# Infini-attention with an FNet layer: the 16 slots of an attention group in another order, odd heads' probabilities in three tiles, and projection maxima taken from SBUF copies

## The chip, the cores and the metric

The kernel runs on one core of a Trainium2 chip. The metric is the device time of one execution in microseconds (us); less is better. Three runs of the kernel before gave 1058.62, 1060.83 and 1062.48 us; the median is 1060.83 us.

## The reference

Two layers on separate inputs, joined along the last axis. A is an Infini-attention with 32 heads of 18 features over four segments of 512 rows; B is a Fourier mixing layer, four dense products. Cut to what is computed:

```python
def _A_ref(x, wq, wk, wv, wo, beta):              # x [1, 2048, 576]
    q, k, v = (per head and segment) x @ wq, x @ wk, x @ wv
    for s in range(4):
        p = softmax(q_s k_s^T * scale + mask)     # 512 x 512, lower triangle
        a_dot = p @ v_s
        a_mem = phi(q_s) @ M / (phi(q_s) @ z + 1e-6)
        o_s = g * a_mem + (1 - g) * a_dot
        M, z = M + phi(k_s)^T v_s, z + sum(phi(k_s))
    return concat(o) @ wo
def _B_ref(x, ...):                               # x [1, 2048, 576]
    a, b = x @ hid_re^T, x @ hid_im^T
    return seq_re @ a - seq_im @ b
return concat([A, B], axis=-1)                    # [1, 2048, 1152]
```

## The kernel before

**Precision.** Most float32 operands are split into a high and a low part (`hi` = a rounded copy made by ACT, `lo` = the difference made by DVE or POOL), and products are the sum of three matmuls, hi·lo, hi·hi and lo·hi.

**Three stages.** First the four segments are projected (`project_qk` for nine 128-row blocks m = 0 to 3, 8, 4 to 7; then `project_v`, `k_natural` and `lookup`), and q, k and v go to DRAM, scaled and cut into two float16 parts. Then comes the attention stage: 32 groups G of four heads (two "halves" of two heads; x = 0 is the even head of a half, x = 1 the odd one) are worked off by the generator `attention()`, and between its pieces the dense work of layer B is put. Last comes the output product.

**Order.** Nothing is scheduled by a compiler: each engine runs its instructions in the order in which the Python code emits them, and waits on semaphores where data or buffers are not there. `later(n, fn)` emits a piece n ticks afterwards. In the projection there is one tick after each block m and each row tile j of v. In the attention stage `attention()` yields 16 times in each step g; each yield is a slot. After a slot's pieces come a tick and a portion of dense work (`dense()`), so many matmuls that the dense work is spread evenly over 34 steps of 16 slots. `on(lag, fn)` calls a piece for group g - lag, so each step holds pieces of three groups.

**The dense work** is fed in chunks of 128x512. `c_load` (L473) loads a chunk with a DMA on SP's queue, `c_cut` (L481) makes `chi` on ACT and, a tick later, `clo` on POOL (L493), two chunks ahead of their use by the matmuls of L631. There are 160 chunks, five to a step.

**A group of heads.** The even heads are computed with keys on the partitions (`t_fill`, `t_exp`, `t_mask`, `t_hi`, `t_lo`: probabilities come out ready for the product with v); they need the row maxima beforehand (`scores(.., 0, ..)`, `s_min`, `maxima`, `maxima_turn`, `maxima_out`, which ends in the small DMA `st<-mt` on SP's queue). The odd heads are computed with queries on the partitions (`scores(.., 1, ..)`, `f_min`, `f_exp`), cut into `hl` (`f_hi` on ACT, `f_lo`), and turned by a transposing DMA on SP's queue (`f_turn`, L1073), before the product with v (`pv`). Rows of 128 queries come in three kinds, `ROWS`: kind 0 is row block 3 (512 keys), kind 1 blocks 0 and 2 (128 and 384), kind 2 block 1 (256).

**Buffers that tie the order.** Scores live in two pairs of PSUM banks, `s` and `t` (`banks`, L1011), used in turn by four blocks of score matmuls in a step; a block has to wait until the readers of the last one are through. `hl`, the float16 tile [128, 2, 1280] of one half's odd head, has `bufs=2`, and a group takes two of them, one for each half: a group's first `f_hi` writes where the group before was, and so waits for that group's `f_turn` to have been read by the DMA. The code that takes it is

```python
        if len(hl) == half:
            hl.append(sa.tile([P, 2, 1280], F16, name="hl", bufs=2))
```

SP's queue issues in order as well: `st<-mt`, the loads of a later group (`stack_load`, four DMAs; `value_load`, one), `c_load`, the stores, and `f_turn`.

**Projection.** `project_qk` (L287) copies a block from PSUM to SBUF on ACT (`x`, L300), lets DVE take the largest magnitude of each row from PSUM (`largest`, L258), and for queries of segments 1 to 3 goes on with `phi` on the same PSUM bank (ACT L217, L218; DVE L220, L221; POOL L222). One tick later `scales` (POOL, L264 to L269) makes a power of two from the maxima, and two or three ticks later `cut_scaled` cuts the block: for keys ACT L278 and DVE L279, for queries ACT L274, L275 and POOL L276; a tick later `keep` issues the two DMAs to DRAM.

Of the kernel before, what the change touches and what calls it, by code (L numbers as in the profile page):

```python
# [24 lines left out]
P = 128  # L25
# [13 lines left out]
def infini_attention_and_fnet(ctx: ExitStack, tc: tile.TileContext, xT, wqk, w8, wv, wo, beta, xtT, cT, hT, out):  # L39
# [231 lines left out]
    def cut_scaled(x, scale, engine):  # L271
        p = sb.tile([P, 2, L], F16, name="p", tag="p", bufs=5)
        if engine is pool:
            act.activation(x, x, AF.Copy, scale=scale)  # L274
            act.activation(p[:, 0], x, AF.Copy)  # L275
            pool.tensor_tensor(p[:, 1], x, p[:, 0], OP.subtract)  # L276
        else:
            act.activation(p[:, 0], x, AF.Copy, scale=scale)  # L278
            dve.scalar_tensor_tensor(p[:, 1], x, scale, p[:, 0], op0=OP.mult, op1=OP.subtract)  # L279
        return p  # L280
# [6 lines left out]
    def project_qk(s, m):  # L287
# [13 lines left out]
        if m < 8:  # L301
            largest(o, MX[m % 4][:, m // 4:m // 4 + 1])
        else:
            t = sb.tile([P, 1], F32, name="mt", bufs=1)
            MX[4] = y = sb.tile([P, 2], F32, name="mx", bufs=5)
            largest(o, t)
# [3 lines left out]
        if m >= 4:  # L310
# [15 lines left out]
            later(2, low)  # L326
            if m < 8:
                later(3, low_query)
# [678 lines left out]
    ROWS = (((3, 0),), ((0, 384), (2, 0)), ((1, 0),))  # L1007
# [41 lines left out]
    def f_exp(G, kind):  # L1049
        nb, _, _, o, g = F_[G]  # L1050
        o = o.pop(kind)
        if kind == 2:
            g += [sa.tile([P, 768], F32, name="pg", bufs=2) for _ in BOTH]
        rows = [i for i, _ in ROWS[kind]]
        b = nb.rearrange("p (h n) -> p h n", h=2)[:, :, rows[0]:rows[-1] + 1:max(1, rows[-1] - rows[0])]
        act.activation(b, b, AF.Copy, bias=LIFT)  # L1056
        for half in BOTH:
            for i, c in ROWS[kind]:
                w = (i + 1) * P
                act.activation(f_cols(G, half, FIRST_COL[i], w), o[half][:, c:c + w], AF.Exp,  # L1060
                               bias=nb[:, 4 * half + i:4 * half + i + 1], scale=-1.0)

    def f_hi(G, half, a, b):
        hl = F_[G][2]
        if len(hl) == half:
            hl.append(sa.tile([P, 2, 1280], F16, name="hl", bufs=2))
        act.activation(hl[half][:, 0, a:b], f_cols(G, half, a, b - a), AF.Copy)

    def f_lo(G, half, engine, a, b):
        hl = F_[G][2]  # L1070
        engine.tensor_tensor(hl[half][:, 1, a:b], f_cols(G, half, a, b - a), hl[half][:, 0, a:b], OP.subtract)  # L1071

    def f_turn(G, half):  # L1073
        PT[G, 1, half] = sa.tile([P, 20, P], F16, name="ptt", bufs=2)
        nc.sync.dma_start_transpose(PT[G, 1, half], F_[G][2][half].rearrange("p a c -> p (a c)"))
# [23 lines left out]
    def t_fill(G, kind, o):  # L1099
        q, k = ST[G % NST]  # L1100
        if kind == 0:
# [110 lines left out]
    def attention():  # L1212
# [3 lines left out]
        for g in range(STEPS):  # L1216
# [4 lines left out]
            for half in BOTH:  # L1221
                on(1, f_hi, half, 512, 1280)
                on(2, t_lo, half, 2, pool)
# [3 lines left out]
            on(0, scores, 1, 0, b)  # L1227
            on(0, scores, 0, 0, a)
            on(2, pv, 1, 1)
            on(0, f_min, 0, b)  # L1230
            on(0, s_min, 0, a)
# [153 lines left out]
```

## Time and profile before

| | |
|---|---|
| profiled execution | 1060.17 us |
| span of its instructions | 1058.0 us |
| median of three other runs | 1060.83 us |
| mean granted TensorE clock | 0.980 |
| DMA traffic | 181.65 MB, 64.4% of 16 engines' span |
| busy in the eight stretches of 22 us from 249 to 425 us, mean of one | PE 21.53, DVE 14.47, ACT 16.33, POOL 14.75 us |

PE is the matmul engine, PEld its weight loads, DVE, ACT and POOL are the vector, scalar and GpSimd engines, SPq is the queue from which SP issues DMAs. A matmul's recorded duration overlaps the next one's, so PE's busy time says when it had work, not how fast it went. The profiled execution lies 0.66 us under the median, and 2.17 us of it lie outside the span.

A line of a timeline gives the start (us), the time (us), engine, line and operation, then output and inputs, and in brackets how long the engine had been idle and what ended it. A line of the waits gives who waited for whom, the total (us), how often, and the longest. A line of the stages gives the stretch, its length, each engine's busy time and instructions, then the granted clock, the DMA engines' share and GB/s.

### The profile page before, as it was taken

How to read it: one execution, taken by the hardware profiler on the slowest of the kernel's cores; microseconds unless marked ns; L12 is line 12 of the kernel's file. 1: busy time of each engine (PE TensorE's matmuls, PEld its weight loads, DVE VectorE, ACT ScalarE, POOL GpSimd, SP SyncE). 2: the span in 40 equal slices, each digit the busy share in tenths (PEclk: the TensorE clock that was granted, in tenths of full speed). 3: DMA queues.
4: the chain of work that ended last, by engine and by line, in shares of the span. 5: the costliest groups of instructions: out<-in, count | busy, mean ns of one | idle time of the engine just before them, and what ended most of it. 6: DMA issues, size and time to landing. Idle time of an engine off the chain costs nothing.

```text
span 1058.0 us, 25597 instructions
## 1 busy us (share of the span) xinstructions
PE 997.1 (94%) x9246; PEld 898.9 (85%) x9246; DVE 697.5 (66%) x1965; ACT 707.8 (67%) x1612; POOL 706.1 (67%) x984
## 2 busy tenths in 40 slices
PE   9998989978999999999898999998989899999998
PEld 8987979878888888888787889987878788888998
DVE  7756757567666566556666667776556667675675
ACT  6856558466787677766777778867656577667342
POOL 0656656467568766776767878866777788777561
PEclk9998999989999999999999999999999999999999
DMA  6524415355556976788757786567798678887463
GB/s 218 181 92 139 160 38 213 114 173 179 139 148 168 201 177 160 166 206 200 181 160 188 181 204 179 158 167 177 196 207 225 175 186 184 203 189 197 116 199 124
DMA packets 282974, 181.65 MB, mean 172 GB/s; under 512 B 204864, under 2 KB 239808, under 8 KB 282816
## 3 DMA queue, kind: packets, MB, share of 16 engines
q1 hardware_dynamic: 282624, 179.88, 64.4%
q8 instruction: 72, 1.18, 0.5%
q14 instruction: 54, 0.44, 0.1%
q10 hardware_dynamic: 224, 0.14, 0.0%
HBM read 94.06 MB, written 44.83 MB: 131 GB/s over the span
## 4 chain that ended last, share of the span: by engine, by line
PE 41%; ACT 17%; POOL 15%; DVE 14%; issue 10%; DMA 2%; POOLq 0%; SPq 0%; DVEq 0%; ACTq 0%
PE d L631 13%; POOL clo L493 5%; ACT pg L1060 4%; DVE s L1031 4%; PE qk L249 4%; POOL hl L1071 4%; PE v L82 2%; PE d L676 2%; PE d L677 2%; PE s L1023 2%; PE d L678 2%; DVE hl L1071 2%; PE t L918 2%; PE pv L1153 2%; DVE plo L1136 2%
## 5 line engine op out<-in xcount | busy, mean ns | idle before, releaser
L493 POOL TENSOR_TENSOR clo<-craw,chi 128x512 fp32r<-128x512 f32 x159 | 209.2, 1317 | 136.4 <-ACT chi L488 130.7
L1031 DVE CUSTOM_DVE_ANT_0 s<-s,causal 128x128 f32<-128x128 f32 (+2 forms) x448 | 203.2, 482 | 146.9 <-PE s L1023 142.5
L631 PE MATMUL d<-wide,chi 128*128 128x288 f32 x1408 | 257.8, 300 | 4.4 <-ACT y L699 3.1
L631 PEld LDWEIGHTS d<-wide,chi 128*128 128x128 f32 x1408 | 211.2, 191 | 5.8 <-ACT y L699 4.1
L631 PE MATMUL d<-wide,clo 128*128 128x288 f32 x704 | 167.3, 304 | 4.9 <-POOL clo L493 4.9
L631 PEld LDWEIGHTS d<-wide,clo 128*128 128x128 f32 x704 | 117.4, 191 | 6.7 <-POOL clo L493 6.6
L631 PE MATMUL d<-ab,chi 128*128 128x288 f32 x640 | 122.6, 302 | 0.0
L488 ACT ACTIVATE chi<-craw 128x512 fp32r<-128x512 f32 x160 | 100.9, 632 | 7.3 <-PE d L631 5.3
L1071 POOL TENSOR_TENSOR hl<-pg,hl 128x768 f16<-128x768 f32 x64 | 104.9, 1662 | 1.1 <-DMA st<-kd 0.8
L631 PEld LDWEIGHTS d<-ab,chi 128*128 128x128 f32 x640 | 99.7, 193 | 0.0
L1120 ACT ACTIVATE pd<-t 128x384 f32<-128x384 f32 (+1 forms) x128 | 64.6, 531 | 38.3 <-PE t L1109 38.0
L631 PE MATMUL d<-ab,clo 128*128 128x288 f32 x320 | 82.2, 306 | 2.4 <-POOL clo L493 2.3
L1023 PE MATMUL s<-st 54*128 54x256 f16 (+3 forms) x448 | 61.8, 290 | 24.0 <-ACT pg L1060 22.8
L1116 ACT ACTIVATE phi<-t 128x384 f16<-128x384 f32 x128 | 60.8, 475 | 29.1 <-PE t L1109 29.0
L1060 ACT ACTIVATE pg<-s,nb 128x128 f32<-128x128 f32 (+1 forms) x192 | 77.1, 474 | 2.1
L676 PE MATMUL d<-wide,chi 128*128 128x288 f32 x256 | 77.8, 304 | 0.5 <-DVE wide L92 0.3
L677 PE MATMUL d<-wide,chi 128*128 128x288 f32 x256 | 75.7, 296 | 0.0
L678 PE MATMUL d<-wide,clo 128*128 128x288 f32 x256 | 75.6, 295 | 0.0
L1129 ACT ACTIVATE phi<-pd 128x512 f16<-128x512 f32 x64 | 40.3, 629 | 48.8 <-POOL pd L1124 48.5
L1056 ACT ACTIVATE nb<-nb 128x2 f32<-128x2 f32 (+1 forms) x96 | 20.1, 210 | 61.4 <-DVE nb L1031 61.2
L82 PE MATMUL v<-wide,xh 128*128 128x288 f32 x256 | 56.9, 315 | 4.3 <-DVE mx L258 4.3
L1136 POOL TENSOR_TENSOR plo<-pd,phi 128x384 f16<-128x384 f32 x64 | 60.2, 961 | 0.6
(298 smaller groups left out, 2708.8 us busy)
## 6 DMA issues: line engine op xcount, KB each, us to landing
craw<-cT SPq DMA_DIRECT2D x128, 256.0 KB
craw<-xtT SPq DMA_DIRECT2D x32, 320.0 KB
vd<-vs SPq DMA_DIRECT2D x16, 440.0 KB
vst<-vd SPq DMA_DIRECT2D x32, 220.0 KB
st<-qd SPq DMA_DIRECT2D x64, 108.0 KB
st<-kd SPq DMA_DIRECT2D x64, 108.0 KB
yd<-y SPq DMA_DIRECT2D x16, 288.0 KB
y<-yd SPq DMA_DIRECT2D x16, 288.0 KB
```

Source lines behind the costliest of these rows:

```text
L82: pe.matmul(o, a, b, start=n == 0, stop=n == len(terms) - 1)
L488: act.activation(hi, raw[:, :4], AF.Copy)
L493: engine.tensor_tensor(lo, raw[:, :4], hi.bitcast(F32), OP.subtract)
L631: pe.matmul(o[h], a, b[:, h * 288:h * 288 + 288], start=start, stop=stop)
L676: pe.matmul(o, xh[:, k], wl[k][:, cs], start=k == 0, stop=False)
L677: pe.matmul(o, xh[:, k], wh[k][:, cs], start=False, stop=False)
L678: pe.matmul(o, xl[:, k], wh[k][:, cs], start=False, stop=False)
L1023: pe.matmul(o[half][:, first + c:first + c + w], q[r, x, i * P:w], k[r, x, :w], start=True, stop=True)
L1031: dve.tensor_tensor_reduce(x, x, CAUSAL[0][:, L - w:], scale=scale, scalar=-LOWEST, op0=OP.add, op1=OP.min, accum_out=into[:, 4 * half + i ...
L1060: act.activation(f_cols(G, half, FIRST_COL[i], w), o[half][:, c:c + w], AF.Exp, bias=nb[:, 4 * half + i:4 * half + i + 1], scale=-1.0)
L1071: engine.tensor_tensor(hl[half][:, 1, a:b], f_cols(G, half, a, b - a), hl[half][:, 0, a:b], OP.subtract)
L1136: engine.tensor_tensor(lo[:, a:b], f, hi[:, a:b], OP.subtract)
```

## The change

Three things are changed. In the projection, `largest` reads the SBUF copy `x` in place of the PSUM bank; `cut_scaled` emits the high part at once and the low part with its DMAs a tick later; and the cut is emitted three ticks after the block (keys had two) in segments 0 to 2, and two ticks after it (queries had three) in segment 3. In the attention stage, the odd heads' probabilities get three float32 tiles by kind (`pf1`, 512 columns; `pf0`, 512; `pf2`, 256) in place of two (512 and 768), with one `f_hi` and one `f_lo` for each kind and half; in kind 1 the row blocks are taken in the other order. And the pieces of a group stand in other slots (the number in brackets is the lag; h is a half):

| slot | before | after |
|---|---|---|
| 0 | f_hi 512:1280 (1), t_lo 2 (2) | t_lo 2 (2) |
| 1 | scores odd 0 and even 0, pv odd h1 (2), f_min 0, s_min 0 | scores odd 1 and even 0, f_min 1, s_min 0, t_hi h0 (2) |
| 2 | f_exp 0, pv_read odd (2), f_lo 512:1280 on POOL (1) | f_turn h0 (1), t_hi h1 (2), pv_out odd (2) |
| 3 | pv_out odd (2) | f_turn h1 (1), f_exp 1, t_lo 0 h0 (2) |
| 4 | f_turn h0 (1) | f_hi 1, t_lo 0 h1 (2) |
| 5 | scores even 1, t_fill 0 (1), pv even h0 (2), s_min 1, t_exp 0 (1) | f_lo 1 on POOL |
| 6 | f_turn h1 (1), t_mask (1) | scores odd 0 and even 1, pv even (2), f_min 0, s_min 1 |
| 7 | - | memory_load (1) |
| 8 | t_hi h0 (1), memory_load (1) | f_exp 0 |
| 9 | scores even 2 and odd 2, t_fill 1 (1), pv even h1 (2), s_min 2, t_exp 1 and t_lo 1 (1), f_min 2, pv_read even (2) | f_hi 0 |
| 10 | maxima, f_exp 2, t_hi h1 and t_lo 0 h0 (1) | scores even 2 and odd 2, t_fill 1 (1), s_min 2, f_min 2, t_exp 1 (1) |
| 11 | pv_out even (2), f_hi 0:512, t_lo 0 h1 (1) | maxima, f_exp 2, t_lo 1 (1), pv_read even (2) |
| 12 | f_lo 0:512 on DVE | f_hi 2, pv_out even (2) |
| 13 | scores odd 1, t_fill 2 (1), maxima_turn, pv odd h0 (1), f_min 1, maxima_out, t_exp 2 (1) | f_lo 2 on POOL, f_lo 0 on DVE |
| 14 | f_exp 1, stack_load, value_load | t_fill 0 and 2 (1), pv odd (1), maxima_turn, t_exp 0 (1), maxima_out, t_exp 2 (1), pv_read odd (1) |
| 15 | - | t_mask (1), stack_load, value_load |

The diff, cut to its core (the new order inside `attention()` is the table's right column):

```diff
@@ -268,16 +268,23 @@
         if c == 4:
             pool.tensor_copy(sc[64:, :1], sc[64:, 1:])
 
-    def cut_scaled(x, scale, engine):
+    def cut_scaled(x, scale, engine, *stores):
         p = sb.tile([P, 2, L], F16, name="p", tag="p", bufs=5)
         if engine is pool:
             act.activation(x, x, AF.Copy, scale=scale)
             act.activation(p[:, 0], x, AF.Copy)
-            pool.tensor_tensor(p[:, 1], x, p[:, 0], OP.subtract)
         else:
             act.activation(p[:, 0], x, AF.Copy, scale=scale)
-            dve.scalar_tensor_tensor(p[:, 1], x, scale, p[:, 0], op0=OP.mult, op1=OP.subtract)
-        return p
+
+        def low():
+            if engine is pool:
+                pool.tensor_tensor(p[:, 1], x, p[:, 0], OP.subtract)
+            else:
+                dve.scalar_tensor_tensor(p[:, 1], x, scale, p[:, 0], op0=OP.mult, op1=OP.subtract)
+            for key, s, rows, part in stores:
+                keep(key, s, rows, p[part])
+
+        later(1, low)
 
     def keep(key, s, rows, p):
         x = (qd, kd)[key][s][rows]
@@ -299,11 +306,11 @@
             x = sb.tile([P, L], F32, name="r", tag="r", bufs=3)
         act.activation(x, o, AF.Copy)
         if m < 8:
-            largest(o, MX[m % 4][:, m // 4:m // 4 + 1])
+            largest(x, MX[m % 4][:, m // 4:m // 4 + 1])
         else:
             t = sb.tile([P, 1], F32, name="mt", bufs=1)
             MX[4] = y = sb.tile([P, 2], F32, name="mx", bufs=5)
-            largest(o, t)
+            largest(x, t)
             for i in range(2):
                 act.activation(y[64 * i:64 * i + 64, 1 - i:2 - i], t[64 - 64 * i:128 - 64 * i], AF.Copy)
                 dve.tensor_copy(y[64 * i:64 * i + 64, i:i + 1], t[64 * i:64 * i + 64])
@@ -311,21 +318,18 @@
             c = m - 4
             later(1, scales, c)
 
-            def low():
-                p = cut_scaled(x, SC[c][:, int(m < 8):2 if m < 8 else 1], dve)
+            def cut_key():
                 if m < 8:
-                    later(1, keep, 1, s, slice(c * P, (c + 1) * P), p)
+                    cut_scaled(x, SC[c][:, 1:], dve, (1, s, slice(c * P, (c + 1) * P), slice(0, P)))
                 else:
-                    later(1, keep, 0, s, slice(512, D), p[:64])
-                    later(1, keep, 1, s, slice(512, D), p[64:])
-
-            def low_query():
-                p = cut_scaled(Q.pop(c), SC[c][:, :1], pool)
-                later(1, keep, 0, s, slice(c * P, (c + 1) * P), p)
-
-            later(2, low)
+                    cut_scaled(x, SC[c][:, :1], dve, (0, s, slice(512, D), slice(0, 64)), (1, s, slice(512, D), slice(64, P)))
+
+            def cut_query():
+                cut_scaled(Q.pop(c), SC[c][:, :1], pool, (0, s, slice(c * P, (c + 1) * P), slice(0, P)))
+
+            later(3 if s < 3 else 2, cut_key)
             if m < 8:
-                later(3, low_query)
+                later(3 if s < 3 else 2, cut_query)
         if s and (m < 4 or m == 8):
             n = P if m < 4 else 64
             c = m if m < 4 else 4
@@ -1004,7 +1008,7 @@
 
 
 
-    ROWS = (((3, 0),), ((0, 384), (2, 0)), ((1, 0),))
+    ROWS = (((3, 0),), ((2, 0), (0, 384)), ((1, 0),))
     FIRST_COL = {3: 0, 2: 512, 0: 896, 1: 1024}
     BOTH = range(2)
 
@@ -1035,44 +1039,44 @@
         smallest(o, kind, -1.0, NEGM[G % 2])
 
     F_ = {}
+    F_COL = (0, 512, 1024, 1280)
 
     def f_min(G, kind, o):
-        if kind == 0:
-            F_[G] = (sa.tile([P, 8], F32, name="nb", bufs=2),
-                     [sa.tile([P, L], F32, name="pf", bufs=2) for _ in BOTH], [], {}, [])
+        if kind == 1:
+            F_[G] = sa.tile([P, 8], F32, name="nb", bufs=2), {}, {}, []
         smallest(o, kind, -SCALE, F_[G][0])
-        F_[G][3][kind] = o
-
-    def f_cols(G, half, a, w):
-        return F_[G][4][half][:, a - L:a - L + w] if a else F_[G][1][half][:, :w]
+        F_[G][1][kind] = o
 
     def f_exp(G, kind):
-        nb, _, _, o, g = F_[G]
+        nb, o, f, _ = F_[G]
         o = o.pop(kind)
-        if kind == 2:
-            g += [sa.tile([P, 768], F32, name="pg", bufs=2) for _ in BOTH]
+        a, b = F_COL[kind:kind + 2]
+        f[kind] = [sa.tile([P, b - a], F32, name=f"pf{kind}", bufs=2) for _ in BOTH]
         rows = [i for i, _ in ROWS[kind]]
-        b = nb.rearrange("p (h n) -> p h n", h=2)[:, :, rows[0]:rows[-1] + 1:max(1, rows[-1] - rows[0])]
-        act.activation(b, b, AF.Copy, bias=LIFT)
+        n = nb.rearrange("p (h n) -> p h n", h=2)[:, :, rows[-1]:rows[0] + 1:max(1, rows[0] - rows[-1])]
+        act.activation(n, n, AF.Copy, bias=LIFT)
         for half in BOTH:
             for i, c in ROWS[kind]:
-                w = (i + 1) * P
-                act.activation(f_cols(G, half, FIRST_COL[i], w), o[half][:, c:c + w], AF.Exp,
+                w, to = (i + 1) * P, FIRST_COL[i] - a
+                act.activation(f[kind][half][:, to:to + w], o[half][:, c:c + w], AF.Exp,
                                bias=nb[:, 4 * half + i:4 * half + i + 1], scale=-1.0)
 
-    def f_hi(G, half, a, b):
-        hl = F_[G][2]
-        if len(hl) == half:
-            hl.append(sa.tile([P, 2, 1280], F16, name="hl", bufs=2))
-        act.activation(hl[half][:, 0, a:b], f_cols(G, half, a, b - a), AF.Copy)
-
-    def f_lo(G, half, engine, a, b):
-        hl = F_[G][2]
-        engine.tensor_tensor(hl[half][:, 1, a:b], f_cols(G, half, a, b - a), hl[half][:, 0, a:b], OP.subtract)
+    def f_hi(G, kind):
+        _, _, f, hl = F_[G]
+        for half in BOTH:
+            if len(hl) == half:
+                hl.append(sa.tile([P, 2, 1280], F16, name="hl", bufs=2))
+            act.activation(hl[half][:, 0, F_COL[kind]:F_COL[kind + 1]], f[kind][half], AF.Copy)
+
+    def f_lo(G, kind, engine):
+        _, _, f, hl = F_[G]
+        for half, x in zip(BOTH, f.pop(kind)):
+            a, b = F_COL[kind:kind + 2]
+            engine.tensor_tensor(hl[half][:, 1, a:b], x, hl[half][:, 0, a:b], OP.subtract)
 
     def f_turn(G, half):
         PT[G, 1, half] = sa.tile([P, 20, P], F16, name="ptt", bufs=2)
-        nc.sync.dma_start_transpose(PT[G, 1, half], F_[G][2][half].rearrange("p a c -> p (a c)"))
+        nc.sync.dma_start_transpose(PT[G, 1, half], F_[G][3][half].rearrange("p a c -> p (a c)"))
 
     def maxima(G):
         m, b = NEGM[G % 2].rearrange("p (h n) -> p h n", h=2), MB[G % 2][:, :24].rearrange("p (h c n) -> p c h n", h=2, c=3)
@@ -1098,7 +1102,7 @@
 
     def t_fill(G, kind, o):
         q, k = ST[G % NST]
-        if kind == 0:
+        if kind == 1:
             for half in BOTH:
                 PT[G, 0, half] = [sa.tile([P, 1280], F16, name="phi", bufs=2), sa.tile([P, 1280], F16, name="plo", bufs=2),
                                   sa.tile([P, 1024], F32, name="pd", bufs=2), None]
@@ -1135,9 +1139,12 @@
         f = (f[:, :512], kept, f[:, 512:896])[kind]
         engine.tensor_tensor(lo[:, a:b], f, hi[:, a:b], OP.subtract)
 
-    def pv(G, x, half):
-        if half == 0:
-            PV[G, x] = ps.tile([P, 440], F32, name="pv", bufs=1)
+    def pv(G, x):
+        PV[G, x] = ps.tile([P, 440], F32, name="pv", bufs=1)
+        for half in BOTH:
+            value_sums(G, x, half)
+
+    def value_sums(G, x, half):
         pt = PT.pop((G, x, half))
         h = 2 * half + x
         for i in range(4):
...
@@ -1218,95 +1225,94 @@
...
+            on(1, f_turn, 0)
+            on(2, t_hi, 1)
             on(2, pv_out, 1)
             yield SLOT
 
-            on(1, f_turn, 0)
+            on(1, f_turn, 1)
+            on(0, f_exp, 1)
+            on(2, t_lo, 0, 0)
+            yield SLOT
+
+            on(0, f_hi, 1)
+            on(2, t_lo, 1, 0)
+            yield SLOT
+
+            on(0, f_lo, 1, pool)
             yield SLOT
...
             a, b = banks("s"), banks("t")
-            on(0, scores, 1, 1, a)
+            on(1, t_fill, 0, a)
             on(1, t_fill, 2, b)
+            on(1, pv, 1)
             t = on(0, maxima_turn, b[0])
-            on(1, pv, 1, 0)
-            on(0, f_min, 1, a)
+            on(1, t_exp, 0, a)
             on(0, maxima_out, t)
             on(1, t_exp, 2, b)
...
```

More of the change, by code (lines that the diff above doesn't have):

```diff
@@ L1219, in on @@
                     return fn(g - lag, *a)
-            for half in BOTH:
-                on(1, f_hi, half, 512, 1280)
-                on(2, t_lo, half, 2, pool)
+            on(2, t_lo, 0, 2, pool)
+            on(2, t_lo, 1, 2, pool)
             yield SLOT
             a, b = banks("s"), banks("t")
[L1227 to L1231, printed above, removed]
-            yield SLOT
-            on(0, f_exp, 0)
-            on(2, pv_read, 1)
-            for half in BOTH:
-                on(1, f_lo, half, pool, 512, 1280)
+            on(0, scores, 1, 1, a)
+            on(0, scores, 0, 0, b)
+            on(0, f_min, 1, a)
+            on(0, s_min, 0, b)
+            on(2, t_hi, 0)
             yield SLOT
@@ L1269, in attention @@
             on(1, t_fill, 1, b)
-            on(2, pv, 0, 1)
             on(0, s_min, 2, e)
+            on(0, f_min, 2, f)
             on(1, t_exp, 1, b)
-            for half in BOTH:
-                on(1, t_lo, half, 1)
-            on(0, f_min, 2, f)
-            on(2, pv_read, 0)
             yield SLOT
@@ L1308, in attention @@
                 value_load(g)
-            yield SLOT
             yield SLOT
```

47 lines of the change are left out of this document (23 added, 24 removed).

## Prediction

> **What bounds the kernel now.** I read the page, then the stages, then the waits of PE.
>
> ```profile
> PE 997.1 (94%) x9246; PEld 898.9 (85%) x9246; DVE 697.5 (66%) x1965; ACT 707.8 (67%) x1612; POOL 706.1 (67%) x984
> ```
> ```profile
> 0.00:248.00 248.00, 228.48 (x1335) 204.71 (x1335) 166.77 (x346) 159.56 (x349) 138.21 (x220) 0.96 0.45 150
> 248.00:957.00 709.00, 673.67 (x7072) 601.66 (x7074) 467.36 (x1491) 504.12 (x1159) 512.77 (x696) 0.99 0.74 181
> ```
> ```profile
> PE s L1023 <- ACT pg L1060: 22.8, 42, 2.5
> PE kt L342 <- ACT kf L300: 7.9, 6, 2.0
> PE d L631 <- POOL clo L493: 7.2, 9, 1.6
> PE v L82 <- DVE mx L258: 4.3, 2, 2.8
> PE d L631 <- ACT y L699: 3.1, 3, 2.2
> PE look L439 <- DVE mx L258: 2.0, 1, 2.0
> ```
>
> PE has work for 94% of the span, 92% in the projection (the first row of the stages) and 95% in the attention stage (the second), so only its idle time and its clock can be won. In the attention stage it idles 709.0 - 673.67 = 35.3 us; 22.8 of that is score matmuls waiting until ACT's `f_exp` has read the s banks. In the projection 7.9 + 4.3 + 2.0 = 14.2 us hang on ACT and DVE.
>
> The clock comes on top. After long gaps it is halved for a while:
>
> ```profile
> core 0: 1058.0 us, clock 0.980
> ```
> ```profile
> 829.48 0.37 PE L1023 MATMUL s<-st 54*128 54x512 f16 x1 [2.54 <-ACT pg L1060]
> ```
> ```profile
> 919.56 0.37 PE L1023 MATMUL s<-st 54*128 54x512 f16 x1 [2.01 <-ACT pg L1060]
> ```
> ```profile
> 90.70:97.50 6.80, 4.76 (x22) 4.64 (x22) 4.53 (x9) 6.32 (x13) 5.18 (x13) 0.50 0.80 229
> 155.60:162.40 6.80, 6.03 (x27) 6.03 (x28) 4.75 (x8) 5.19 (x12) 4.43 (x11) 0.50 0.86 265
> 223.80:230.70 6.90, 5.22 (x23) 5.22 (x24) 4.99 (x14) 6.18 (x14) 4.67 (x10) 0.51 0.96 331
> 527.60:531.00 3.40, 3.40 (x37) 2.65 (x36) 3.33 (x11) 2.33 (x7) 0.31 (x1) 0.50 0.40 151
> 831.40:834.80 3.40, 3.40 (x17) 3.40 (x16) 0.51 (x2) 3.37 (x8) 3.40 (x5) 0.50 0.36 115
> 920.20:923.60 3.40, 3.31 (x29) 2.80 (x29) 2.19 (x8) 3.37 (x8) 2.77 (x2) 0.50 1.04 336
> ```
>
> The two gaps over 2 us on a bank, and the one of 2.2 us on `y` in the waits, which ended at 526.9, are each followed by a stretch of 3.4 us at clock 0.50 (the last three rows), which costs half its length. A mean clock of 0.980 is 2% of the span, 21 us; the first three rows, 20.5 us at half clock, are 10 of these (8 if only the 16.0 us in which PE had work count), so some 10 us are left for the attention stage.
>
> The last number wanted is the length of a step.
>
> ```profile
> L1023 PE MATMUL s<-st x448: 212/280/581, 248.3 to 956.9; 54*128 54x256 f16 x43, 54*128 54x384 f16 x43, 54*128 54x128 f16 x42, 54*128 54x512 f16 x22
> ```
>
> From the first score matmul (slot 1 of step 0) to the last (slot 13 of step 31) are 31.75 steps: 708.6 / 31.75 = 22.3 us a step. Without gaps and half clock PE would need (673.67 - 10) / 31.75 = 20.9.
>
> **The change: projection.** The blocked chain, in segment 1:
>
> ```profile
> 87.65 0.72 ACT L278 ACTIVATE p<-kf,sc 128x512 f16<-128x512 f32 x1 [3.57 <-POOL sc L269]
> ```
> ```profile
> 92.86 0.48 PE L342 MATMUL kt<-ident,kf 128*128 128x128 f32 x1 [2.04 <-ACT kf L300]
> ```
> ```profile
> ACT qe L217 <- DVE mx L258: 15.0, 12, 1.5
> ```
>
> ACT stands 3.57 us at the cut, waiting for a scale from POOL; behind it in ACT's queue are the copies of the next key blocks, and the transposes of `k_natural` wait for those. The change moves the cut behind one more copy, and its low part with its DMAs another tick on. It also takes out the wait in the last row: with `largest` on the SBUF copy, ACT no longer waits for DVE between its copy and `phi`, since only ACT and the end of `phi` still read the bank. So ACT stops lagging, the scales come earlier, and banks come free sooner. No instruction is added; the reduction from SBUF I take at its old length, and off the path even if it were half or double. Segment 3 keeps its key cut at two ticks and moves the query cut forward to two; ACT may still stand there for POOL, but earlier, while PE has four blocks left. Of the 14.2 us I take 12, and of the 8 us of clock 6: **-18 us** (from -6, if POOL's scales still hold ACT, to -22).
>
> **The change: attention, what is removed.** The s banks written in slot 1 are wanted again in slot 6, not three slots after a queue of exponentials, and the next ones after four, four and three slots. With `f_exp` two slots after its scores the 22.8 us should go, and with them most of the clock's 10.
>
> **What is added, small.** `f_lo` on POOL is cut from 768 to 512 and 256 columns, `f_hi` from 768 and 512 to 512, 512 and 256: one fixed part more per half on each.
>
> ```profile
> L1071 POOL TENSOR_TENSOR hl<-pg,hl 128x768 f16<-128x768 f32 x64 | 104.9, 1662 | 1.1 <-DMA st<-kd 0.8
> ```
>
> The row gives 1.66 us at 768 columns. The extra fixed part is at least nothing and at most a third of it, 0.55 us, for each half; I take a half of that, +0.5 us a step on POOL, and the same as a bound for ACT. Both engines idle over 25% in this stage, so alone this costs nothing. From the same row, 512 columns on POOL take at least two thirds of 1.66, 1.1 us, and I count 1.2 for `f_lo` and 1.3 for `clo`, an operation of the same width (estimates).
>
> **What is added, large: a loop through `hl`.** Before, `f_hi` first writes a group's `hl` in slot 11, long after the group before was turned (slots 4 and 6). After, `f_turn` is issued from slots 2 and 3 and the next group's `f_hi` writes the same two buffers in slot 4. The wait exists already, with almost no slack:
>
> ```profile
> 725.81 6.91 DMA ptt<-hl
> ```
> ```profile
> 732.75 0.64 ACT hl L1067
> ```
> ```profile
> 722.01 2.57 SPq L1075 DMA_TRANSPOSE ptt<-hl  x1
> ```
>
> In the chain of work the second turn, issued at 725.81, is through 6.91 us later, and ACT starts `f_hi` just then. From the first issue (722.01) both took 10.71 us. So where do the turns stand on SP's queue?
>
> ```profile
> 397.19 1.52 SPq L92 DMA_DIRECT2D st<-mt  x2
> ...
> 401.11 1.03 SPq L478 DMA_DIRECT2D craw<-cT  x2
> ...
> 406.50 2.58 SPq L1075 DMA_TRANSPOSE ptt<-hl  x1
> ...
> 409.81 2.77 SPq L1075 DMA_TRANSPOSE ptt<-hl  x1
> ```
>
> Behind `st<-mt`, the loads and a chunk or two: 402.14 - 397.19, less half a chunk, 4.5 us. There the turns waited on (402.1 to 406.5) until POOL had made the last part of `hl`; after the change that is made in slot 13, before the loads, so they go out right behind them. And `st<-mt` waits for `maxima_out` on ACT, which in ACT's queue stands ten slots behind `f_hi`. That closes a circle of one step: f_hi, ACT's queue and PE to `maxima_out`, SP's queue, the turns, the next f_hi. Its length, from the end of the second half's f_hi:
>
> ```profile
> 403.36 0.22 ACT L1056 ACTIVATE nb<-nb 128x2 f32<-128x2 f32 x1
> 403.61 1.27 ACT L1060 ACTIVATE pf<-t,nb 128x512 f32<-128x512 f32 x2
> ```
> ```profile
> 410.44 0.39 PE L1023 MATMUL s<-st 54*128 54x256 f16 x4
> ```
> ```profile
> 415.62 0.39 PE L1023 MATMUL s<-st 54*128 54x128 f16 x4
> ```
> ```profile
> 416.11 0.23 PE L1087 MATMUL t<-ident,mb 128*128 128x128 bf16 x1
> ```
> ```profile
> 401.55 0.37 PE L1023 MATMUL s<-st 54*128 54x512 f16 x1 [0.15 <-ACT pg L1060]
> ```
> ```profile
> 402.39 0.51 PE L631 MATMUL d<-wide,clo 128*128 128x288 f32 x2
> ```
>
> - held-up chunks on ACT (five a step, so 1.25 in slots 4 to 7; at most 0.64 us each, the length of an `f_hi` of the same 512 columns in the chain above): 0.7 us
> - `f_exp` 0: 403.61 + 1.27 - 403.36 = 1.5
> - slots 10 to 14 on PE, which can only start its scores when `f_exp` 0 has freed the bank: 415.62 - 410.44 = 5.2 for a block and four slots, less the half `pv` that moves out (0.5: the last two rows, 0.84 us apart, hold one score matmul and such a half), plus the block of slot 14 (two fills, 0.5, as scores and a fill took from 415.62 to 416.11; both halves of `pv`, 1.0; the turn, 0.2) and `maxima_out`, 0.4 with its start: 6.8
> - SP to the first turn: 4.5
> - both turns: at least 3.31 + 2.77 = 6.1 (issue to issue and the second's own issue), at most 10.7 as above; I take the middle, 8.4
> - the second half's `f_hi`: 0.7
>
> That is 22.6. While ACT stands, the chunks behind it stand, and POOL's `f_lo` 1 stands in front of their `clo`; a chunk cut in slots 4 or 5 is wanted four slots later and holds PE in slots 8 and 9 until `f_lo` and `clo` (1.2 and 1.3 as above) are done, 0.4 us after `f_exp` 0, with up to 1.8 us of dense work still ahead of slot 10: 0.8 on average. The circle is 23.4 us, PE idles 2.5 us in each step in one or two gaps, and if half of these bring a half clock, at 1.7 us in slots 10 to 13, which are part of the circle, it is 24.2. Thirty-one steps times 24.2 - 22.3: **+59 us**.
>
> A rule bears on this last term. The Trainium skill, "TensorE: Matmul & The Clock Gate", section "Why this matters for your kernels", asks for no idle gap over about 3 us; by it gaps of 2.5 us would leave the clock alone, the circle would stay at 23.4 and the sum at 1076. The three gaps of 2.0 to 2.5 us above speak against it.
>
> **Sum.** 1060.2 - 18 + 59 = **1101 us** for the profiled kind of execution; the median of the runs shown is 0.7 us above that, which is left out.
>
> **Rivals.**
> - *The circle does not close* (faster). If both turns take near 6.1 us it is 21.1 us long, as long as PE's own step, and ACT only loses idle time. Then 1060 - 18 - 22 (bank waits) - 6 (clock) + 4 (chunks cut late) = **1018 us**. For it: the low bound is a row. Against: the pair at 722.01 took 10.7, and after the change the turns go out right behind five loads. The Trainium skill, "DMA: Bandwidth & Descriptors", section "Latency and other measured facts", gives 261 GB/s for a transposing DMA; an estimate by it is 2.5 us for 0.66 MB, which would favour this rival, and the 6.91 us above speaks against it.
> - *It closes only just*: both turns in 7.3 us, no half clock: 22.3 us a step, as now, and the projection's gain stays: 1060 - 18 = **1042 us**.
> - *It closes hard*: turns in 9.5 us and a half clock in each step: 23.4 + 1.1 + 1.7 = 26.2: 1060 - 18 + 31 x 3.9 = **1163 us**. For it: every gap over 2 us brought the half clock.
> - *The projection does not gain*: POOL still holds ACT; 12 us on top of any of these.
>
> **How the numbers follow.** The circle of 23.4 us stands 2.5 us over PE's 20.9, and its widest term, the turns, is uncertain by 2.3 us to either side; so that it closes is likely, not sure. Forecast (1065 to 1140) 0.46, hard 0.11, just (1035 to 1065) 0.12, not closed (1005 to 1035) 0.31. A difference of 0.3%, 3.2 us, is what can be told from none. Slower: 0.46 + 0.11 + 0.01 = 0.58; same 0.03; faster 0.31 + 0.08 = 0.39. The forecast's own range is 1065 to 1140; the range that leaves out 0.2 lets the hard case go and the lowest quarter of the open one: 1012 to 1140.
>
> **What would show it.** Right: ACT's `f_hi` of kind 1 waiting for `ptt<-hl` some 4 to 6 us in each step, PE's waits on `clo` and on `f_exp` 0 in place of those on `pg` L1060 in slot 1, a step of 23 to 25 us, and in the projection no wait of `kt` on `kf`. Wrong: `f_hi` without that wait, or ACT standing and PE not; then the step is 21 to 22 us and the first rival holds.

## The result and the profile after

The change makes the kernel slower: 1206.16 us (median of 4 runs, 1204.63 to 1213.07; a fifth took 1201.69) against 1061.23 us, a ratio of 1.137 (95% interval 1.132 to 1.142). The forecast was 1101, with 1012 to 1140 as its range. The profiled execution of the changed kernel took 1213.07 us, its span 1211.4.

The page's first rows, the stages and the mean clock of the changed kernel:

```profile
PE 1047.5 (86%) x9246; PEld 947.3 (78%) x9246; DVE 715.8 (59%) x1965; ACT 715.8 (59%) x1676; POOL 731.9 (60%) x1048
```
```profile
0.00:242.00 242.00, 227.44 (x1339) 203.43 (x1339) 170.05 (x344) 159.77 (x349) 137.40 (x219) 0.97 0.45 152
242.00:1097.00 855.00, 715.36 (x6977) 641.49 (x6978) 474.72 (x1476) 506.75 (x1210) 531.74 (x749) 0.89 0.64 149
```
```profile
core 0: 1211.4 us, clock 0.913
```

No engine is the bound any more: PE falls from 94% to 86%, and all others fall too. The attention stage now starts at 241.2 us (248.3 before) and holds the whole loss. Its score matmuls run from slot 1 of step 0 to slot 10 of step 31, which are 31.56 steps:

```profile
L1027 PE MATMUL s<-st x320: 216/366/418, 241.2 to 1106.8; 54*128 54x256 f16 x64, 54*128 54x384 f16 x32, 54*128 54x128 f16 x32, 54*128 54x512 f16 x32
```

(1106.8 - 241.2) / 31.56 = 27.4 us a step, where there were 22.3. The waits say where:

```profile
ACT hl L1069 <- DMA ptt<-hl: 237.3, 62, 8.6
POOL hl L1075 <- ACT hl L1069: 215.0, 63, 10.0
...
PE s L1027 <- ACT pf L1061: 63.3, 33, 5.4
PEld d L635 <- ACT chi L492: 47.8, 9, 7.2
```

ACT waits for the turning DMA in each of the 31 steps, for both halves (62 times), 237.3 us in all, or 7.7 us a step. PE waits behind it: for the bank that `f_exp` reads, and (the last row, of its weight loads) for chunks whose `chi` stands behind `f_hi` in ACT's queue. This is the circle through `hl` that the prediction described. One turn of it, from SP's queue, the chain of waits and ACT's and PE's timelines:

```profile
507.34 7.85 SPq L1079 DMA_TRANSPOSE ptt<-hl  x2
...
529.44 1.53 SPq L92 DMA_DIRECT2D st<-mt  x2
...
534.56 4.44 SPq L1079 DMA_TRANSPOSE ptt<-hl  x1
```
```profile
512.13 4.95 DMA ptt<-hl
```
```profile
517.16 0.63 ACT L1069 ACTIVATE hl<-pf 128x512 f16<-128x512 f32 x1 [2.64 <-DMA ptt<-hl]
...
518.43 1.27 ACT L1061 ACTIVATE pf<-s,nb 128x512 f32<-128x512 f32 x2
...
529.05 0.36 ACT L1096 ACTIVATE mt<-t,inverse 24x128 f16<-24x128 f32 x1 [0.28 <-PE t L1091]
```
```profile
521.08 0.61 PE L1027 MATMUL s<-st 54*128 54x256 f16 x4
```

The second turn, issued 4.8 us after the first, has landed at 517.1; at 517.16 ACT makes the second half's `f_hi`, then `f_exp` 0 (done at 519.70); PE starts slot 10 at 521.08; `maxima_out` runs at 529.05, the maxima's DMA goes out at 529.44, and behind the loads the next first turn at 534.56, 27.2 us after the last. The terms beside the prediction's; the mean is of the differences between the same events in 26 steps, from the turn at 321.9 us on (the 27.4 above is over all steps, the first ones included):

| term of the circle, us | predicted | step at 507.34 | mean of 26 |
|---|---|---|---|
| first turn issued to second landed | 8.4 | 9.7 | 10.5 |
| second half's `f_hi`, with its start | 0.7 | 0.7 | 0.7 |
| to the end of `f_exp` 0 (with held-up chunks) | 2.2 | 1.9 | 2.3 |
| to PE's first score of slot 10 (late chunks) | 0.8 | 1.4 | 0.5 |
| to the end of `maxima_out` (with half clock) | 7.6 | 8.3 | 8.6 |
| to the next first turn | 4.5 | 5.2 | 4.9 |
| step | 24.2 | 27.2 | 27.6 |

So 31 x (27.6 - 22.3) = +164 us, less 7 for the earlier start: 1060 + 157 = 1217, beside 1213 measured.

### The profile page after: what moved, and what is told of

Its sections match the earlier page's. It is cut to its first block, busy times and chain, and to the rows that moved or that the text cites. A ratio compares the mean times of both kernels' runs of the same rounds, so it can differ in the third digit from the quotient of the medians.

```text
span 1211.4 us, 25894 instructions
## 1 busy us (share of the span) xinstructions
PE 1047.5 (86%) x9246; PEld 947.3 (78%) x9246; DVE 715.8 (59%) x1965; ACT 715.8 (59%) x1676; POOL 731.9 (60%) x1048
## 4 chain that ended last, share of the span: by engine, by line
PE 61%; DMA 17%; ACT 7%; POOL 6%; DVE 4%; issue 3%; SPq 2%; POOLq 0%; ACTq 0%; DVEq 0%
PE d L635 27%; DMA ptt<-hl 14%; PE qk L82 4%; PE qk L249 4%; PE pv L1160 3%; PE d L680 3%; PE s L1027 3%; PE d L681 2%; PE d L682 2%; POOL clo L497 2%; PE t L922 2%; ACT pf L1061 2%; PE pv L1161 1%; ACT chi L492 1%; PE v L82 1%
## 5 line engine op out<-in xcount | busy, mean ns | idle before, releaser
L635 PE MATMUL d<-wide,chi 128*128 128x288 f32 x1408 | 280.8, 320 | 31.7 <-ACT chi L492 20.9
L1035 DVE CUSTOM_DVE_ANT_0 s<-s,causal 128x384 f32<-128x384 f32 (+2 forms) x320 | 147.2, 501 | 257.8 <-PE s L1027 155.4
L635 PEld LDWEIGHTS d<-wide,chi 128*128 128x128 f32 x1408 | 233.0, 209 | 41.2 <-ACT chi L492 22.0
L1075 POOL TENSOR_TENSOR hl<-pf,hl 128x256 f16<-128x256 f32 (+1 forms) x128 | 121.8, 962 | 215.3 <-ACT hl L1069 215.0
L1069 ACT ACTIVATE hl<-pf 128x512 f16<-128x512 f32 (+1 forms) x192 | 100.0, 558 | 237.3 <-DMA ptt<-hl 237.3
L635 PE MATMUL d<-wide,clo 128*128 128x288 f32 x704 | 180.4, 325 | 3.5 <-POOL clo L497 3.5
L1061 ACT ACTIVATE pf<-s,nb 128x384 f32<-128x384 f32 (+3 forms) x256 | 117.7, 527 | 3.1
L1027 PE MATMUL s<-st 54*128 54x256 f16 (+3 forms) x320 | 48.9, 335 | 63.3 <-ACT pf L1061 63.3
L1035 DVE CUSTOM_DVE_ANT_0 t<-t,causal 128x384 f32<-128x384 f32 (+1 forms) x192 | 98.9, 542 | 2.2
L680 PE MATMUL d<-wide,chi 128*128 128x288 f32 x256 | 82.3, 322 | 18.5 <-DVE wide L92 16.4
L1027 PEld LDWEIGHTS <-st 54*128 54x128 f16 x512 | 20.8, 96 | 91.7 <-issue 85.3
L681 PE MATMUL d<-wide,chi 128*128 128x288 f32 x256 | 79.3, 310 | 0.0
L682 PE MATMUL d<-wide,clo 128*128 128x288 f32 x256 | 79.3, 310 | 0.0
L680 PEld LDWEIGHTS d<-wide,chi 128*128 128x128 f32 x256 | 51.5, 201 | 23.6 <-DVE wide L92 17.8
L635 PEld LDWEIGHTS d<-ab,clo 128*128 128x128 f32 x320 | 59.5, 206 | 5.0 <-POOL clo L497 3.0
```

The costliest lines, as they stand in the source:

```text
L635: pe.matmul(o[h], a, b[:, h * 288:h * 288 + 288], start=start, stop=stop)
L680: pe.matmul(o, xh[:, k], wl[k][:, cs], start=k == 0, stop=False)
L681: pe.matmul(o, xh[:, k], wh[k][:, cs], start=False, stop=False)
L682: pe.matmul(o, xl[:, k], wh[k][:, cs], start=False, stop=False)
L1027: pe.matmul(o[half][:, first + c:first + c + w], q[r, x, i * P:w], k[r, x, :w], start=True, stop=True)
L1035: dve.tensor_tensor_reduce(x, x, CAUSAL[0][:, L - w:], scale=scale, scalar=-LOWEST, op0=OP.add, op1=OP.min, accum_out=into[:, 4 * half + i ...
```

## The experiments

The theory is this circle; the rival is that the new order of banks and slots costs PE the time, with or without the wait on the turns. Each ratio is to the kernel before, run on the same chip; line numbers are each kernel's own, those of the attention stage four higher where the projection's part is in.

### The two parts alone

The projection part alone on the kernel before, then the attention part alone:

> The kernel before with the change's projection part only; the attention stage is as it was. Reading of the two traces: the attention stage begins at 241.2 us in place of 248.3, so 7 us less, 1054 us (the prediction had said 18 less, 1042). Rival: the earlier start is given back in an attention stage that waits on the same things as before, or on stores to DRAM that now come a tick later: no change, 1061 us.

> The change's attention part only, with the projection of before. If the two parts do not touch each other, this is the changed kernel plus the 7 us that its projection won: 1213 us. Rival: the later projection stores of the change hold up the first groups' loads, and part of the 145 us comes from there: under 1190 us.

Measured: 1055.51 us (0.9941, 0.9918 to 0.9964) and 1211.52 us (1.1393, 1.1352 to 1.1435). The parts add up: the projection wins 6 us, the attention part loses 150. The rivals, an earlier start that is given back and stores that hold up the first groups' loads, are out.

### The turns in their own step

From slots 2 and 3 to slot 14, a step earlier (lag 0 for 1):

```diff
-            on(1, f_turn, 0)
...
-            on(1, f_turn, 1)
...
             on(1, pv, 1)
+            for half in BOTH:
+                on(0, f_turn, half)
             t = on(0, maxima_turn, b[0])
```

> The changed kernel with both turns issued in slot 14 of their own step, ahead of the maxima's DMA and of the loads, in place of slots 2 and 3 of the next step. Theory (the circle f_hi, maxima_out, SP's queue, turns, f_hi): maxima_out and SP's 4.9 us drop out of it, the turns have landed about slot 5 to 6 and f_hi of kind 1 waits 0 to 2 us, ahead of slots that ACT can catch up in; PE's own work sets the step at 21 to 22 us: 1020 to 1050 us. Rival (the order of the s and t banks, not the turns, makes the loss): f_hi no longer waits, but PE still waits on f_exp 0 in slot 10: over 1150 us.

Measured: 1076.83 us (1.0152, 1.0121 to 1.0183), a step of 23.1 us. 129 us came back with no bank moved, so the rival falls; but it is not the 1020 to 1050 expected. In this kernel's waits (attention stage) the wait on the turns has shrunk to 42.1 us, and a new one stands beside it, the first row:

```profile
ACT chi L492 <- DMA craw<-cT: 80.7, 24, 7.3
ACT hl L1069 <- DMA ptt<-hl: 42.1, 30, 4.4
```

SP's timeline shows why:

```profile
646.49 7.30 SPq L1079 DMA_TRANSPOSE ptt<-hl  x2
653.89 1.54 SPq L92 DMA_DIRECT2D st<-mt  x2
...
657.15 0.59 SPq L553 DMA_DIRECT2D vst<-vd  x1
657.78 1.09 SPq L482 DMA_DIRECT2D craw<-xtT  x2
```
```profile
662.97 0.63 ACT L492 ACTIVATE chi<-craw 128x512 fp32r<-128x512 f32 x1 [5.29 <-DMA craw<-xtT]
```

Two turns, the maxima and the five loads in one block keep SP's queue for 11.3 us (646.49 to 657.78); the chunk loads behind them come late, and ACT stands 5.29 us for one, again ahead of `f_exp` 0.

### A third buffer for `hl`

(The later stages that use the same buffers take three as well.)

```diff
-                hl.append(sa.tile([P, 2, 1280], F16, name="hl", bufs=2))
+                hl.append(sa.tile([P, 2, 1280], F16, name="hl", bufs=3))
...
-        a = sa.tile([P, 8, DH], F32, name="pa", bufs=2)
+        a = sa.tile([P, 8, DH], F32, name="pa", bufs=1)
```

> The changed kernel with hl in three buffers in place of two (and the small tile pa in one, to make room). The first f_hi of a group then waits for nothing recent, and the second for the first of the turns before, which lands 6 us after it is issued, in place of the second, 10.5 us after. Theory: 4.5 us leave the circle of 27.6 us; it is 23.1 us, still over PE's 21, and the time falls by 31 x 4.5 = 140 us to about 1067 us, less if PE's gaps become too short to halve the clock. Rival (bank order): no change, 1206 us.

Measured: 1071.16 us (1.0092, 1.0062 to 1.0122), a step of 23.1 us, where 1067 and 23.1 were expected. ACT now waits once in a step in place of twice:

```profile
ACT hl L1069 <- DMA ptt<-hl: 134.2, 31, 7.9
```

Which of two turns `f_hi` waits for is what differs in the circle (`pa` is not part of it), and it is worth 135 us. Four buffers, with which no wait would be left, were not tried: already the third took a buffer from `pa`.

### Where the wait stands, and what SP issues ahead of the turns

First edit: `f_hi` 1 from slot 4 to 9, `f_lo` 1 from 5 to 10, `f_hi` 0 from 9 to 12. Second edit: the loads from slot 15 to slot 4 of the next step.

```diff
-            on(0, f_hi, 1)
-            on(0, f_lo, 1, pool)
...
-            on(0, f_hi, 0)
+            on(0, f_hi, 1)
...
+            on(0, f_lo, 1, pool)
...
+            on(0, f_hi, 0)
```
```diff
+            if g:
+                stack_load(g + 1)
+                value_load(g - 1)
...
-            stack_load(g + 2)
-            if g < NG:
-                value_load(g)
```

> The changed kernel with f_hi of kind 1 in slot 9 (behind f_exp 0), f_lo of kind 1 in slot 10 and f_hi of kind 0 in slot 12; the turns stay in slots 2 and 3 and hl keeps two buffers, so the wait on the turns stays in ACT's queue but no longer stands ahead of f_exp 0 and of the chunks of slots 4 to 8. Theory (where the wait stands in ACT's queue makes the loss): the turns land about slot 10, ACT waits some 1 to 2 us in slot 9, the next things behind it are t_exp 1 and f_exp 2, wanted in slot 14: the step is 21 to 23 us, 1015 to 1080 us. Rival (the length of the circle alone counts, wherever the wait stands): the circle loses only PE's slots 4 to 9, and f_exp 2 then holds the banks of slot 14, so that the step stays over 25 us: over 1125 us.

> The changed kernel with the five loads of a later group moved from slot 15 to slot 4, behind the two turns in SP's queue; everything else as changed. Theory: of the 4.9 us from the maxima's DMA to the first turn some 2.4 us (five issues) leave the circle; the step goes from 27.6 to 25.2 us: 1130 us. Rival (the turns wait for f_lo or for PE's pv to free their target, not for SP's queue): no change, 1206 us.

> Both of the last two edits. Theory: the turns land 2.4 us sooner, about slot 8, so f_hi of kind 1 in slot 9 waits hardly at all; PE's own 21 us and the bank waits that are left set the step: 1005 to 1050 us. Rival (ACT's queue in slots 8 to 13 is now too full, f_exp 2 comes too late for slot 14): PE waits there 1 us or more in each step, over 1060 us.

> The later f_hi together with the third hl buffer. Theory: the wait on the turns is gone altogether; what is left is PE's 21 us and ACT's crowding in slots 8 to 13: 1005 to 1050 us, and the difference from the run before this one tells what the remaining wait on the turns costs. Rival as there: over 1060 us.

| run | us | ratio (95%) | step, us |
|---|---|---|---|
| changed kernel | 1206.16 | 1.137 (1.132 to 1.142) | 27.4 |
| `f_hi` behind `f_exp` | 1072.04 | 1.0086 (1.0059 to 1.0113) | 22.9 |
| loads behind turns | 1089.75 | 1.0262 (1.0223 to 1.0300) | 23.6 |
| both | 1017.05 | 0.9582 (0.9547 to 0.9616) | 21.2 |
| `f_hi` behind, third `hl` | 1017.70 | 0.9591 (0.9554 to 0.9628) | 21.3 |

(The step is worked out as above, from the first and last `s` score.) With `f_hi` behind `f_exp` alone both sides of its expectation came true in part: the step fell under 23 us, but the wait moved to slot 14, as the rival said. The waits of this kernel in the attention stage:

```profile
ACT hl L1069 <- DMA ptt<-hl: 83.1, 43, 5.0
...
PE s L1113 <- ACT pf L1061: 20.3, 26, 4.4
```

The second row is `t_fill` waiting for the banks of `f_exp` 2, which is late because ACT stands for the turns in slot 9.

The loads were worth more than their 2.4 us. Read as in the table of the circle, the way from the maxima to the first turn fell by 2.5 us (4.9 to 2.4), as expected; and besides, the second turn is issued 0.6 us sooner after the first (4.3 us for 4.9), and slots 10 to 14 take 0.9 us less, with a mean clock of 0.962 for 0.913 over the span. My expectation left those two out.

With both edits ACT waits for the turns 16 times in the whole stage, and PE has work for 632 of 650 us:

```profile
ACT hl L1069 <- DMA ptt<-hl: 24.4, 16, 3.2
```
```profile
250.00:900.00 650.00, 631.83 (x6862) 572.68 (x6861) 466.52 (x1435) 492.32 (x1191) 530.51 (x733) 0.99 0.79 190
```

The later `f_hi` with the third buffer ends at the same step. Its wait was expected to be gone altogether; it is not:

```profile
ACT hl L1069 <- DMA ptt<-hl: 20.2, 13, 3.1
```

The wait comes 16 and 13 times in these two runs, where the changed kernel had it 62 times, and it no longer sets the step, which is 21.2 or 21.3 us with PE's own 20.9: the bank order of the change is good, and the kernel takes 1017 to 1018 us once the circle is open.

### The projection, part by part

```diff
-            largest(o, MX[m % 4][:, m // 4:m // 4 + 1])
+            largest(x, MX[m % 4][:, m // 4:m // 4 + 1])
...
-            largest(o, t)
+            largest(x, t)
```

> The kernel before with one edit: largest reads the SBUF copy. Theory (ACT's copy and phi no longer wait for DVE's maximum, 15.0 us of ACT's idle time in the projection; the later cut is what gives half of that back by holding the p buffers): this edit alone wins as much as the whole projection part or more, 6 to 12 us: 1050 to 1055 us. Rival (the wait for POOL's scales at the key cut, L278, holds ACT whatever largest reads): 0 to 3 us, 1058 to 1062 us.

The cuts alone are the rest of the change's projection part, with `largest` on PSUM:

> The kernel before with the other edit of the projection part: cuts a tick later for keys (a tick earlier in segment 3 for queries), low part and stores a tick after the high part; largest reads PSUM as before. Theory (the cut's timing gives back part of what largest wins, because a p tile is held longer and three ACT instructions of a key's and a query's cut now stand in one tick): no gain or a loss, 1058 to 1066 us. Rival (the later cut removes the wait for POOL's scales and is the part that wins): 1050 to 1056 us.

And the projection part with one number changed:

```diff
-                later(3 if s < 3 else 2, cut_query)
+                later(2, cut_query)
```

> The projection part alone (1055.5 us), with the query cut at two ticks in all segments, the key cut still at three: the three ACT instructions no longer fall in one tick, and ACT's waits on stores of p (about 5 us in the projection part alone) may fall. Theory: PE's waits on vr, which stand behind them, go in part: 1050 to 1054 us. Rival (p tiles are held as long as before, and the query cut now stands for POOL's scales): 1055 to 1060 us.

Measured: `largest` alone 1048.21 us (0.9870, 0.9857 to 0.9883), the cuts alone 1071.62 us (1.0090, 1.0076 to 1.0103), the query cut sooner 1057.48 us (0.9962, 0.9949 to 0.9975). So `largest` wins 13.5 us, more than the 6 to 12 expected, and the cuts lose 9.9, more than the 1066 us expected at most. The two do not just add up (3.6 us, where both together win 6.0): beside `largest`, the cuts cost 7.3. The last run is a miss: spreading the cuts over two ticks does not help, and ACT's waits for stores of `p`, 5.1 us in the projection part alone, are 10.4 us instead of less.

In the run of `largest` alone, PE's wait `kt` on `kf` is 0.6 us where it was 7.9, though ACT still stands as long for POOL's scale:

```profile
ACT p L278 <- POOL sc L269: 10.8, 3, 3.6
```
```profile
84.05 0.72 ACT L278 ACTIVATE p<-kf,sc 128x512 f16<-128x512 f32 x1 [3.58 <-POOL sc L269]
```

The same wait, 3.57 us, ended at 87.65 before; here it ends at 84.05, 3.6 us sooner, because ACT's 15.0 us of waiting for DVE's maxima are gone. That was the cure; the wait for the scale needed none. PE's own waits for the maxima (`v` 4.3, `look` 2.0) are gone too. Up to the first score, which comes 12.0 us sooner (236.3 for 248.3), PE stands idle for 11.4 us instead of 19.4, and the half clock lasts 6.8 us instead of 20.5: 8.0 us of the gain are idle time, and the other 4 are work that takes less time with less half clock.

In the run of the cuts alone, ACT's timeline shows what they cost:

```profile
173.64 0.72 ACT L277 ACTIVATE p<-kf,sc 128x512 f16<-128x512 f32 x1 [1.34 <-DMA qd<-p]
174.27 0.71 ACT L274 ACTIVATE q<-q,sc 128x512 f32<-128x512 f32 x1
175.00 0.63 ACT L275 ACTIVATE p<-q 128x512 f16<-128x512 f32 x1
175.54 0.61 ACT L57 ACTIVATE xh<-raw 128x512 fp32r<-128x512 f32 x1
176.06 0.41 ACT L365 ACTIVATE vs<-v 128x288 bf16<-128x288 f32 x1
```
```profile
178.73 0.38 PE L443 MATMUL look<-md,pq_hi 128*128 128x304 f32 x1 [2.69 <-DVE vr L368]
```

A `p` tile is now wanted while the store of an older one is still under way (1.34 us), and a cut stands in front of `xh` and of the value rows' `vs` and `vn`; DVE's `xl`, `vn` and `vr` follow these in order, and PE, which needs the bank that `vr` reads, stands 2.69 us. In that run PE waits 4.7 us with `look` L443 for `vr`, where it had been 0.6, and 1.7 with `qk` for `xt`; `kt` on `kf` only falls from 7.9 to 3.9, and ACT's 15.1 us for DVE's maxima stay. The attention stage starts 8.2 us later (256.5): PE's idle time up to there grows by 4.3 us, and the rest goes with the half clock (23.9 us of it for 20.5) in work that takes longer. But `look` waits more for `vr` in the run of `largest` alone as well (6.5 us for 1.7), so that wait is not the cuts' doing alone. More `p` buffers were not tried, so how much is due to the buffers and how much to the order on ACT stays open.

### What is left, together

The attention stage with both edits, and of the projection part `largest` alone:

> The attention stage of the run with both edits (f_hi of kind 1 behind f_exp 0, loads behind the turns), and in the projection only the edit of largest, with the cuts timed as before the change. If the parts add up: 1017 us, less what the later cuts cost beside largest (1055.5 - 1048.2 = 7.3 us): 1010 us. Rival (in the changed order of the attention stage an earlier start only lengthens a wait there): 1017 us.

Measured: 1009.17 us (0.9516, 0.9496 to 0.9535), 4.8% less than the kernel before and 16% less than the changed one; 1010 was expected. The page's first row of this kernel and its score matmuls:

```profile
PE 970.0 (96%) x9246; PEld 884.0 (88%) x9246; DVE 719.5 (72%) x1965; ACT 707.3 (70%) x1676; POOL 743.6 (74%) x1048
```
```profile
L1023 PE MATMUL s<-st x320: 216/280/387, 232.4 to 902.2; 54*128 54x256 f16 x64, 54*128 54x384 f16 x32, 54*128 54x128 f16 x32, 54*128 54x512 f16 x32
```

The stage starts at 232.4 us, 15.9 sooner than before, and a step takes (902.2 - 232.4) / 31.56 = 21.2 us, near the 20.9 that the prediction worked out for PE without gaps.

## Why the prediction was right or wrong

- **The mechanism of the attention part: right.** ACT's `f_hi` of kind 1 waits for `ptt<-hl` in every step, and of PE's waits behind it the one on `f_exp` 0 is as named (63.3 us). The other was named on `clo` and is on `chi`: PE waits 45.7 us with its matmuls for chunks that ACT has not cut yet, and only 4.7 for `clo`. Three ways of shortening or moving the wait (a third buffer, the loads, the place of `f_hi`) each give back 116 to 135 us.
- **Its size: wrong, by three terms.** The step came out at 27.6 us, not 24.2. The step of the prediction that failed is "I take the middle, 8.4" for both turns: they take 10.5 us, near the upper bound of 10.7 that its own row showed. It is 2.1 of the 3.4 us that were missing. The low bound, 6.1, was no bound: it counts the second turn as done when SP has issued it, but a turn lands about 2 us after that (median 2.1 us in the kernel before, 1.9 in the changed one, by the semaphore's updates). Counted to the landing, the pairs of the kernel before took 6.9 to 11.8 us, median 8.7, so that 8.4 fits the old places and not the new ones. The time goes with what stands right ahead of the turns in SP's queue: with the queue idle ahead of them (turns in slot 14) the median is 8.6 us, behind the maxima's DMAs and a chunk (loads behind turns) 9.5, and behind the five loads as well (changed kernel) 10.4. That the turns go out right behind five loads stood in the prediction as an argument against the low bound, and was not followed into the sum. Slots 10 to 14 with `maxima_out` took 8.6 us instead of 7.6, and SP's way to the first turn 4.9 instead of 4.5. Each 0.1 us counts 31 times; a term of a circle that is off by 2.1 us is off by 65 us in the time.
- **The range: too narrow above.** "Lets the hard case go" left out 1163 us, and the result lies above even that. The three largest terms all came out above the value taken; the sum with each upper bound had not been made. With 10.7 for the turns and a half clock in each step it is 23.4 + 2.3 + 1.7 = 27.4 us, or 1200 us in all.
- **The half clock: about right in the circle.** Slots 10 to 14 take 8.6 us here and 7.6 us, read in the same way, with both edits, where the clock is 0.99 in this stage: 1.0 us, with 0.8 predicted. It was reckoned to come in half of the steps; the mean clock of this stretch is under 0.9 in 23 of 29 steps of the changed kernel, and in 1 of 28 with both edits. So most of what this term was short of is not clock: at full clock the stretch takes 7.6 us (as in the changed kernel's own steps from 712.88 and 743.88 us, at clock 1.00), where the prediction counted 6.8. That the clock is only 0.89 over the whole stage does not add to that: PE's dense work outside slots 10 to 14 is not on the circle.
- **What is removed, and the small additions: right, but only seen with the circle open.** With both edits the waits on the banks that led the list before are 2.1 us, and the third `f_hi` and `f_lo` cannot cost more than the 0.3 us between a step of 21.2 us and PE's 20.9.
- **The projection: -18 predicted, -6 measured.** The step that failed is "The change moves the cut behind one more copy, and its low part with its DMAs another tick on", counted as a part of the gain. It loses 9.9 us by itself and 7.3 beside `largest`. The other step, "ACT no longer waits for DVE between its copy and `phi`", wins 13.5 us alone, near the 18 given for the whole. The rival "the projection does not gain" was not the case either, and not for its reason: POOL does still hold ACT, and that costs PE next to nothing: its wait of `kt` on `kf` is gone in the changed kernel, as foretold.
- **The first rival** was refused for good reason in this order (no pair of turns takes 6.1 us). That its price of 1018 us is what the open circle measures, 1017.05, is luck: it took 18 us for the projection, which gave 6, and 24 for the attention stage, which gives 38 (1055.51 - 1017.05) once the circle is open.

## What to carry to other kernels

When a group's first write comes close behind the last read of the same buffer one step earlier, follow the buffer's circle through every queue and add it up with each term at its upper bound; if that exceeds the step, find the cheapest place to cut it: here a copy moved behind the exponentials and five loads moved behind two DMAs. A wait in an in-order queue costs what stands behind it, so where it stands can be worth as much as its length. Test the parts of a change one by one: 13.5 us won by one and 7 to 10 lost by the other looked like one small gain.

## What the runs showed of the hardware

A turning DMA keeps SP's queue longer when other DMAs stand right in front of it. Its issues, minimum, median and longest in ns, in the kernel before and in the changed one:

```profile
L1075 SPq DMA_TRANSPOSE ptt<-hl x64: 2442/2841/5499, 273.8 to 969.5; - x64
```
```profile
L1079 SPq DMA_TRANSPOSE ptt<-hl x64: 3021/3932/5736, 266.1 to 1123.5; - x64
```

Before, SP's queue stood idle ahead of 31 of the 32 first turns of a group, and their median issue is 2.6 us; after, each goes out within 0.3 us of another DMA, mostly behind all five loads, and the median is 4.4 us. With the loads moved behind the turns it is 3.7, and with both turns in slot 14, behind an idle queue, 3.2. The second turn of a group has another DMA right ahead of it in all of these; its median is 3.0 us before and 3.6 after.

The matmul clock halves after shorter gaps than the page of the Trainium skill that the prediction cites allows ("TensorE: Matmul & The Clock Gate", section "Why this matters for your kernels", about 3 us). Over the fourteen profiles of this case, of 65 gaps of 2.0 to 2.5 us in which neither matmuls nor weight loads ran, 57 were followed by a half clock that began no later than 3.5 us behind the gap; of 146 gaps of 1.0 to 2.0 us, only 38. Some of the latter may belong to a longer gap close by.
